# The last rows: each accumulator copied by two engines, and one transfer for each half over four batches

## Chip, cores and metric

The kernel runs on one core of a Trainium2 chip. Its time is the device time of one execution in microseconds (us). Times inside a profile count from the first instruction of the profiled execution.

## What is computed

There are 8 batches, each with 512 tokens and 32 state rows, in 8 heads of 64. The tokens read the state by attention and the state reads the tokens; the two results are put together as 544 rows of 512 for each batch. Every row then goes through the same two-layer network.

```python
scores = scale * np.matmul(x, state.transpose(0, 1, 3, 2))     # (8, 8, 512, 32)
xread = np.matmul(softmax(scores), state)                      # 512 rows of each batch
scores2 = scale * np.matmul(state, x.transpose(0, 1, 3, 2))    # (8, 8, 32, 512)
sread = np.matmul(softmax(scores2), x)                         # 32 rows of each batch
x = concatenate([xread, sread], axis=2) ...reshape(8 * 544, 512)
h = x @ w_in                                                   # (4352, 2048)
g = np.where(h <= -1, 0, np.where(h >= 1, h, (h + 1) ** 2 / 4))
out = g @ w_out                                                # (4352, 512), float32
```

Rows 544 b to 544 b + 511 of `out` are batch b's tokens, rows 544 b + 512 to 544 b + 543 its state rows.

## The kernel before

The kernel goes through nine steps: the tokens of batches 0 to 7, and then, as b = B = 8, the state rows of all eight batches together, 8 x 32 = 256 rows. In each step the hidden units are taken in groups. `g1` (line 504) makes a group's hidden values in PSUM and squares and bounds them on ScalarE and VectorE; `g2` (line 515) multiplies them with `w_out` and adds to accumulators of 128 rows x 512 columns (`acc[b][t]`), four for a batch's tokens and two (t = 0 and 1) for the state rows. Each product is done in three matmuls (lines 534 to 536) of values split in a high and a low part. The loop at line 807 does `g1` of a group, prepares the next one and then does `g2` of the group before; line 825 does the last `g2`.

In the last group of a step the matmuls are sorted by accumulator (line 525), so accumulator 0 is finished first, and `store` (line 542) is called as each is finished. In the last step that is 12 matmuls for accumulator 0, its `store`, 12 matmuls for accumulator 1, its `store`, and then the program ends. `store` copies the accumulator from PSUM into a tile `o` in SBUF and writes it to `out` by DMA. For tokens (b < 8) ScalarE copies, and one transfer of 128 rows goes out on ScalarE's own queue. For the state rows, accumulator t holds 32 rows of each of the batches 4 t to 4 t + 3, which lie 544 rows apart in `out`. Accumulator 0 is copied by ScalarE, accumulator 1 by VectorE (line 546), each as 512 columns, and then four transfers of 32 rows, 64 KB each, go out, two on ScalarE's queue (ACT) and two on SyncE's (SP).

The order of instructions on each engine is the order of the code in this part. A planner with costs (class `Plan`) orders only the first batch. Waits between engines are put in by the tile layer, which tracks the accesses of each tile. The end of the program (line 865) is SyncE waiting for the last transfers, and a drain of all engines.

Of the kernel before, what the change touches and what calls it, by code (L numbers as in the profile page):

```python
# [137 lines left out]
def state_exchange_moe(  # L138
# [17 lines left out]
    nc = tc.nc  # L156
    B, P, NT, H, D = x.shape
    S = NT * P
    NS = 32
    DM = H * D  # L160
# [6 lines left out]
    TOK = S + NS  # L167
# [283 lines left out]
    acc = {}  # L451
# [63 lines left out]
    def g2(b, j, half=None):  # L515
        n = n_of[b]
        per = S // n
        nt = n // P
        if b not in acc:
            acc[b] = [ps_acc(f"acc{b}_{t}") for t in range(nt)]  # L520
        gh, gl = gs[b, j]
        last = j == NJ // per - 1
        pairs = [(i, t) for i in range(2 * per) for t in range(nt)]
        if last:
            pairs.sort(key=lambda p: p[1])
        if half is not None:
            pairs = pairs[half * len(pairs) // 2:][:len(pairs) // 2]
        for i, t in pairs:
            f = 2 * per * j + i
            oh, ol = wo[f // 2][:, 0, f % 2], wo[f // 2][:, 1, f % 2]  # L530
            c0 = (i % per) * n + t * P
            lh, ll = (v[:, i // per, c0:c0 + P] for v in (gh, gl))
            a = acc[b][t]
            nc.tensor.matmul(a, lhsT=lh, rhs=oh, start=f == 0, stop=False)  # L534
            nc.tensor.matmul(a, lhsT=lh, rhs=ol, start=False, stop=False)  # L535
            nc.tensor.matmul(a, lhsT=ll, rhs=oh, start=False, stop=f == NF - 1)  # L536
            if last and i == 2 * per - 1:
                store(b, t)
# [3 lines left out]
    def store(b, t):  # L542
        if t == 0:
            outs[b] = rawp.tile([P, NT, DM], F32, tag="raw", name=f"o{b}")
        o = outs[b][:, t]
        if b == B and t % 2:
            nc.vector.tensor_copy(o, acc[b][t])
        else:
            nc.scalar.copy(out=o, in_=acc[b][t])  # L549
        if b < B:  # L550
            r0 = b * TOK + t * P
            nc.scalar.dma_start(out=out[r0:r0 + P, :], in_=o)
        else:
            for i in range(4):
                r0 = (4 * t + i) * TOK + S
                (nc.sync if i % 2 else nc.scalar).dma_start(
                    out=out[r0:r0 + NS, :], in_=o[i * NS:(i + 1) * NS]
                )

# [307 lines left out]
```

## Time and profile before

| | us |
|---|---|
| median of 3 runs | 663.96 (663.55 to 664.05) |
| the profiled execution | 664.0 |
| its span, first to last instruction | 662.2 |
| TensorE matmul busy | 653.9 |
| ScalarE / VectorE busy | 356.5 / 340.3 |
| HBM read / written | 34.08 MB / 8.91 MB |

The profile shows one execution. Engines are PE (TensorE matmul), PEld (its weight load), ACT (ScalarE), DVE (VectorE), POOL (GpSimd) and SP (SyncE); a q behind the name means the engine's sequencer, which issues DMAs and waits. A timeline row gives the start, the duration, the engine, the line of the kernel and the operation with its tiles; idle time before it and what ended it stand in brackets. A row of windows gives, for a stretch of time, each engine's busy time, the granted clock of TensorE, the mean busy share of the 16 DMA engines, and the GB/s that they moved. What ended an idle time is inferred by the profiler.

### The profile page before, as it was taken

How to read it: one execution, taken by the hardware profiler on the slowest of the kernel's cores; microseconds unless marked ns; L12 is line 12 of the kernel's file. 1: busy time of each engine (PE TensorE's matmuls, PEld its weight loads, DVE VectorE, ACT ScalarE, POOL GpSimd, SP SyncE). 2: the span in 40 equal slices, each digit the busy share in tenths (PEclk: the TensorE clock that was granted, in tenths of full speed). 3: DMA queues.
4: the chain of work that ended last, by engine and by line, in shares of the span. 5: the costliest groups of instructions: out<-in, count | busy, mean ns of one | idle time of the engine just before them, and what ended most of it. 6: DMA issues, size and time to landing. Idle time of an engine off the chain costs nothing.

```text
span 662.2 us, 10304 instructions
## 1 busy us (share of the span) xinstructions
PE 653.9 (99%) x4442; PEld 514.2 (78%) x4442; DVE 340.3 (51%) x490; ACT 356.5 (54%) x462; POOL 0.8 (0%) x7
## 2 busy tenths in 40 slices
PE   8999999999999999999999999999999999999997
PEld 6677777777787777777787777777778777778896
DVE  5999947623673239433563338433563343333431
ACT  4899847544554446544554447444653454454642
POOL 0000000000000000000000000000000000000000
PEclk9999999999999999999999999999999999999999
DMA  8986103010301003010301002010100000000101
GB/s 359 400 359 249 64 10 119 0 65 0 120 10 64 1 4 124 0 65 0 128 1 64 1 24 105 0 65 0 65 1 1 1 33 32 1 1 1 63 1 33
DMA packets 11085, 43.65 MB, mean 66 GB/s; under 512 B 1312, under 2 KB 1440, under 8 KB 7968
## 3 DMA queue, kind: packets, MB, share of 16 engines
q1 hardware_dynamic: 6096, 34.28, 13.6%
q10 hardware_dynamic: 4944, 8.72, 3.5%
q8 instruction: 35, 0.57, 0.3%
q14 instruction: 10, 0.08, 0.0%
HBM read 34.08 MB, written 8.91 MB: 65 GB/s over the span
## 4 chain that ended last, share of the span: by engine, by line
PE 91%; ACT 5%; DVE 3%; issue 0%; DMA 0%; POOL 0%; SPq 0%; ACTq 0%; POOLq 0%
PE acc L534 19%; PE acc L536 18%; PE acc L535 18%; PE h L477 9%; PE h L479 9%; PE h L478 9%; PE sw L417 5%; PE sc L253 1%; PE sr L350 1%; PE e2p L333 1%; PE warmed L198 1%; ACT u L482 1%; ACT u L485 1%; ACT raw_i L588 1%; DVE w L596 1%; ACT wo L603 0%
## 5 line engine op out<-in xcount | busy, mean ns | idle before, releaser
L534 PE MATMUL acc<-wo,gh 128*128 128x512 f32 x544 | 218.8, 402 | 0.0
L535 PE MATMUL acc<-wo,gh 128*128 128x512 f32 x544 | 212.3, 390 | 0.0
L536 PE MATMUL acc<-wo,gl 128*128 128x512 f32 x544 | 212.2, 390 | 0.0
L482 ACT ACTIVATE u<-h,half 128x512 f32<-128x512 f32 x136 | 93.7, 693 | 219.9 <-PE h L479 202.6
L488 DVE SCALAR_TENSOR_TENSOR u<-u,h 128x512 f32<-128x512 f32 x136 | 87.0, 680 | 206.7 <-ACT u L485 206.7
L534 PEld LDWEIGHTS acc<-wo,gh 128*128 128x128 f32 x544 | 102.1, 188 | 40.1 <-ACT u L482 12.8
L536 PEld LDWEIGHTS acc<-wo,gl 128*128 128x128 f32 x544 | 102.1, 188 | 22.5 <-issue 0.4
L535 PEld LDWEIGHTS acc<-wo,gh 128*128 128x128 f32 x544 | 102.2, 188 | 19.4 <-DVE wo L607 0.3
L502 DVE TENSOR_TENSOR gl<-u,gh 128x1024 fp32r<-128x1024 f32 x68 | 83.2, 1224 | 33.0 <-ACT gh L497 32.0
L497 ACT CAST gh<-u 128x1024 fp32r<-128x1024 f32 x68 | 71.8, 1056 | 50.3 <-DVE u L488 49.9
L485 ACT ACTIVATE u<-u 128x1024 f32<-128x1024 f32 x68 | 72.5, 1065 | 1.3
L417 PE MATMUL sw<-w,sb 64*32 64x256 f32 x1024 | 36.0, 383 | 1.8 <-DVE w L596 1.3
L417 PEld LDWEIGHTS sw<-w,sb 64*32 64x32 f32 x1024 | 15.1, 106 | 17.9 <-issue 8.8
L479 PE MATMUL h<-atl,sw_0h 128*128 128x512 f32 x60 | 23.6, 393 | 0.3 <-DVE atl L306 0.2
L477 PE MATMUL h<-ath,sw_0h 128*128 128x512 f32 x60 | 23.5, 394 | 0.0
L549 ACT COPY o<-acc 128x512 f32<-128x512 f32 x33 | 18.6, 586 | 9.1 <-PE acc L536 9.0
L478 PE MATMUL h<-ath,sw_0l 128*128 128x512 f32 x60 | 23.5, 391 | 0.0
L479 PE MATMUL h<-atl,sw_6h 128*128 128x512 f32 x60 | 23.4, 389 | 0.0
L479 PE MATMUL h<-atl,sw_2h 128*128 128x512 f32 x60 | 23.4, 389 | 0.0
L477 PE MATMUL h<-ath,sw_2h 128*128 128x512 f32 x60 | 23.3, 389 | 0.0
L478 PE MATMUL h<-ath,sw_2l 128*128 128x512 f32 x60 | 23.3, 389 | 0.0
L477 PE MATMUL h<-ath,sw_4h 128*128 128x512 f32 x60 | 23.3, 389 | 0.0
(174 smaller groups left out, 735.0 us busy)
## 6 DMA issues: line engine op xcount, KB each, us to landing
xt<-in_xt_dram SPq DMA_DIRECT2D x16, 512.0 KB, 4.5
raw_i<-in_moe_w_in_dram SPq DMA_DIRECT2D x8, 1024.0 KB, 6.9
raw_o<-in_moe_w_out_dram SPq DMA_DIRECT2D x8, 1024.0 KB, 9.4
xn<-in_x_dram SPq DMA_DIRECT2D x8, 1024.0 KB, 6.4
out_dram<-o ACTq DMA_DIRECT2D x32, 256.0 KB, 2.0
sb<-in_state_dram SPq DMA_DIRECT2D x1, 448.0 KB, 12.6
out_dram<-o SPq DMA_DIRECT2D x4, 64.0 KB, 1.7
out_dram<-o ACTq DMA_DIRECT2D x4, 64.0 KB, 2.0
```

The source lines that it names most:

```text
L417: nc.tensor.matmul(pt[pr * NS:(pr + 1) * NS, hh, i * CI:(i + 1) * CI], lhsT=sb[rows, b, pr], rhs=w32[c + i][rows, pr], start=True, stop=True,)
L477: nc.tensor.matmul(o, lhsT=wh[:, k, sl], rhs=ah[:, k], start=first, stop=False)
L478: nc.tensor.matmul(o, lhsT=wl[:, k, sl], rhs=ah[:, k], start=False, stop=False)
L479: nc.tensor.matmul(o, lhsT=wh[:, k, sl], rhs=al[:, k], start=False, stop=last)
L482: nc.scalar.activation(out=self.u[:, i], in_=self.hs[i], func=AF.Relu, scale=0.5, bias=half)
L485: nc.scalar.activation(out=self.u, in_=self.u, func=AF.Square)
L488: nc.vector.scalar_tensor_tensor(out=self.u[:, i], in0=self.u[:, i], scalar=1.0, in1=self.hs[i], op0=ALU.min, op1=ALU.max,)
L497: nc.scalar.copy(out=gh, in_=self.u)
L502: nc.vector.tensor_tensor(out=gl, in0=self.u, in1=gh.bitcast(F32), op=ALU.subtract)
L534: nc.tensor.matmul(a, lhsT=lh, rhs=oh, start=f == 0, stop=False)
L535: nc.tensor.matmul(a, lhsT=lh, rhs=ol, start=False, stop=False)
L536: nc.tensor.matmul(a, lhsT=ll, rhs=oh, start=False, stop=f == NF - 1)
```

## The change

Only `store` is changed, and in it only the last step. Both accumulators are treated alike: ScalarE copies columns 0 to 255 and VectorE columns 256 to 511. Each half is then written by one transfer of 128 KB, the left on ScalarE's queue and the right on SyncE's. `rows` is a view of `out` with the four batches outermost, then 32 rows, then the columns; the source side of a transfer is 128 partitions x 256 columns.

```diff
         o = outs[b][:, t]
-        if b == B and t % 2:
-            nc.vector.tensor_copy(o, acc[b][t])
-        else:
+        if b < B:
             nc.scalar.copy(out=o, in_=acc[b][t])
-        if b < B:
             r0 = b * TOK + t * P
             nc.scalar.dma_start(out=out[r0:r0 + P, :], in_=o)
         else:
-            for i in range(4):
-                r0 = (4 * t + i) * TOK + S
-                (nc.sync if i % 2 else nc.scalar).dma_start(
-                    out=out[r0:r0 + NS, :], in_=o[i * NS:(i + 1) * NS]
-                )
+            rows = out.rearrange("(b t) d -> b t d", b=B)[4 * t:4 * t + 4, S:S + NS]
+            lo, hi = slice(0, DM // 2), slice(DM // 2, DM)
+            nc.scalar.copy(out=o[:, lo], in_=acc[b][t][:, lo])
+            nc.vector.tensor_copy(o[:, hi], acc[b][t][:, hi])
+            nc.scalar.dma_start(out=rows[:, :, lo], in_=o[:, lo])
+            nc.sync.dma_start(out=rows[:, :, hi], in_=o[:, hi])
```

## Rows read from the trace of the kernel before

**Rows 1.** Page, busy time, share of the span and instructions of each engine.

```profile
PE 653.9 (99%) x4442; PEld 514.2 (78%) x4442; DVE 340.3 (51%) x490; ACT 356.5 (54%) x462; POOL 0.8 (0%) x7
```

**Rows 2.** Chain that ended last, the tail: start us, us, what.

```profile
656.37 1.70 DMA out_dram<-o
```

**Rows 3.** Timeline, end of each accumulator and its copy: start us, us, what.

```profile
654.92 0.39 PE L536 MATMUL acc<-wo,gl 128*128 128x512 f32 x1
...
655.35 0.59 ACT L549 COPY o<-acc 128x512 f32<-128x512 f32 x1 [3.96 <-PE acc L536]
...
657.64 0.39 PE L536 MATMUL acc<-wo,gl 128*128 128x512 f32 x1
658.07 0.69 DVE L547 COPY o<-acc 128x512 f32<-128x512 f32 x1 [5.42 <-DMA out_dram<-o]
```

**Rows 4.** Timeline, first and last DMA issue behind that copy.

```profile
658.78 0.32 SPq L556 DMA_DIRECT2D out_dram<-o  x1
...
659.20 0.44 ACTq L556 DMA_DIRECT2D out_dram<-o  x1
```

**Rows 5.** Windows: engines' busy us, then PEclk, DMA share and GB/s.

```profile
1.60:1.80 0.20, 0.20 (x1) 0.20 (x2) 0.00 (x0) 0.20 (x1) 0.00 (x0) 1.00 0.58 102
...
617.40:617.50 0.10, 0.10 (x2) 0.10 (x1) 0.10 (x1) 0.00 (x0) 0.00 (x0) 1.00 0.56 225
...
616.50:622.00 5.50, 5.50 (x39) 5.11 (x38) 2.29 (x3) 2.73 (x6) 0.00 (x0) 1.00 0.49 191
...
655.90:658.50 2.60, 2.13 (x10) 1.43 (x8) 0.43 (x1) 0.04 (x1) 0.00 (x0) 1.00 0.39 101
...
659.60:659.70 0.10, 0.00 (x0) 0.00 (x0) 0.00 (x0) 0.00 (x0) 0.00 (x0) 1.00 0.77 205
660.70:660.80 0.10, 0.00 (x0) 0.00 (x0) 0.00 (x0) 0.00 (x0) 0.00 (x0) 1.00 0.11 21
...
658.50:662.20 3.70, 0.00 (x0) 0.00 (x0) 0.26 (x1) 0.00 (x0) 0.00 (x0) 1.00 0.27 71
```

**Rows 6.** Line 865 from 659.75 us: durations in ns (min/median/max), first and last start.

```profile
L865 SPq EVENT_SEMAPHORE  x2: 207/730/1252, 659.7 to 661.0; - x2
```

**Rows 7.** Timeline of batch 7's stores: two copies in a row, the first issue.

```profile
615.97 1.07 ACT L549 COPY o<-acc 128x512 f32<-128x512 f32 x2
...
616.58 0.34 ACTq L552 DMA_DIRECT2D out_dram<-o  x1
```

**Rows 8.** Groups by line and shape: xcount | busy us, mean ns | idle before.

```profile
L549 ACT COPY o<-acc 128x512 f32<-128x512 f32 x33 | 18.6, 586 | 9.1 <-PE acc L536 9.0
L337 ACT COPY e<-e2p 128x1024 f32<-128x1024 f32 x8 | 8.1, 1015 | 0.0
...
L502 DVE TENSOR_TENSOR gl<-u,gh 128x1024 fp32r<-128x1024 f32 x68 | 83.2, 1224 | 33.0 <-ACT gh L497 32.0
L547 DVE COPY o<-acc 128x512 f32<-128x512 f32 x1 | 0.7, 692 | 5.4 <-DMA out_dram<-o 5.4
L260 DVE STREAM_TRANSPOSE z<-sc 128x256 f32<-128x256 f32 x4 | 1.6, 429 | 6.5 <-PE sc L253 6.5
```

**Rows 9.** Timeline at 48 us: two engines that read the scores of batch 1.

```profile
48.34 0.72 DVE L260 STREAM_TRANSPOSE z<-sc 128x512 f32<-128x512 f32 x1 [0.91 <-ACT e L322]
...
49.09 0.69 ACT L322 ACTIVATE e<-sc,nm 128x512 f32<-128x512 f32 x1 [0.78 <-DVE z L260]
```

**Rows 10.** DMA queues (SP is q1, ACT q10), and issues: xcount, KB, us to landing.

```profile
q1 hardware_dynamic: 6096, 34.28, 13.6%
q10 hardware_dynamic: 4944, 8.72, 3.5%
...
out_dram<-o ACTq DMA_DIRECT2D x32, 256.0 KB, 2.0
...
out_dram<-o ACTq DMA_DIRECT2D x4, 64.0 KB, 2.0
sb<-in_state_dram ACTq DMA_DIRECT2D x1, 64.0 KB, 4.3
```

## The prediction

> **What bounds the kernel now.** I read the page first: TensorE is busy for 653.9 us of a span of 662.2, so anything that leaves TensorE's work as it is can act only before its first or behind its last matmul [rows 1]. The change sits behind the last, so next come the chain of waits and the timeline of the last 8 us. The chain leaves TensorE early and goes through a copy, a DMA issue and a landing that ends at 658.07 into the last copy [rows 2], and the timeline names the same DMA as that copy's releaser. This has to be doubted. The last matmul of that accumulator runs 657.64 + 0.39 = 658.03, and the copy starts 0.04 us behind it, just as ScalarE's copy of the first accumulator starts 0.04 behind its own (654.92 + 0.39 = 655.31, copy at 655.35) [rows 3]. I take TensorE as the releaser.
>
> From there the tail is: VectorE's copy 658.07 to 658.76 [rows 3]; two transfers on each queue, the first issued at 658.78, the last at 659.20 [rows 4]; their data moves from about 659.61 to 660.8 [rows 5]; SyncE's two last waits for landings, 1.252 us from 659.7 and 0.207 from 661.0, end at 661.2 [rows 6]; the closing steps fill the rest to 662.2. So from the last data to the end of the span it is 1.4 us, 0.4 of them to the last landing. From an issue to its first data it is about 0.84: 658.78 to the slice at 659.60, and 616.58 to the slice at 617.40 for a store in mid-run [rows 5, 7]. The whole tail is 4.2 us.
>
> **The change, copies.** No copy of 256 columns is in the trace. ScalarE takes 586 ns for 512 columns and 1015 for 1024, 0.84 ns a column, so 0.37 us for 256. VectorE takes 692 for 512 and 1224 for 1024, 1.04 ns a column, so 0.43, and its 256-column transposes take 429 ns [rows 8]. Side by side both halves would be out by 658.50. But both read the same accumulator, and the trace has two such readers of one score tile: VectorE's transpose at 48.34 waits for ScalarE's exponential, and the next exponential at 49.09 for that transpose (48.34 + 0.72 = 49.06), though both only read the scores and write different tiles [rows 9]. So I put the halves one behind the other, ScalarE first as the code has it: ScalarE 658.07 to 658.44, VectorE 658.48 to 658.91. The left half is out 0.32 us earlier than now, the right 0.15 later. Bounds for the right half: 658.50 (together) and 658.91.
>
> **Issues.** Each accumulator has two transfers instead of four, so the second issue on each queue goes. An issue follows its copy by 0.02 us (658.76 to 658.78): ACT at 658.46, SP at 658.93, where the last is at 659.20 now. Their data can start at 659.30 and 659.77. First accumulator: ScalarE copies 655.35 to 655.72, issue at 655.74, data from 656.58; VectorE copies 655.76 to 656.19, issue at 656.21, data from 657.05. Behind these on ScalarE, VectorE and SP nothing is queued that TensorE needs: its remaining matmuls write the other accumulator, and both engines are idle until it ends.
>
> **Transfer.** This decides. Now a transfer moves 32 rows of 2 KB; then 128 half rows of 1 KB, and its write side counts four batches outermost and 32 rows within. First the price of a half row. Four stores of 128 full rows in mid-run take 0.49 of 5.5 us of 16 engines, 0.674 us each for eight rows per engine: 0.084 us a row. The last two accumulators, as many bytes in four transfers each, take 0.39 x 2.6 = 1.01 and 0.27 x 3.7 = 1.00 us [rows 5]: three more transfers cost 0.33, so closing one costs up to 0.11, and a row is 0.0705 to 0.084. A half row lies between half of the lower, 0.035, and the whole of the higher, 0.084. Long rows show little cost per row: SP's queue (34.28 MB in 6096 packets) and ACT's (8.72 MB in 4944) both come to some 42 ns of engine time per KB, 13.6% and 3.5% of 16 x 662.2 us [rows 10]. That would make a half row 0.042. The slice with the 512-byte rows of the state load has 0.58 x 0.2 x 16 = 1.86 engine-us for 20 KB, 91 ns per KB [rows 5], and a line through 512 bytes at that rate (0.046) and 2 KB at 0.082 gives 0.058. That slice holds the cold start of the loads too, so I take 0.048, nearer the lower.
>
> Second, over how many engines a transfer is dealt when four is outermost: no row shows it. Every transfer in the trace counts 128 or 32 outermost, which sixteen divides, and is closed on all sixteen: ACT's 32 + 4 + 1 = 37 transfers have 32 x 128 + 4 x 32 + 128 = 4352 rows, and its 4944 packets are 592 = 37 x 16 more [rows 10]. Four can't be dealt evenly over sixteen. The bounds are sixteen engines (the first rival) and, if each outermost step is one share, four; one engine, the far end, would give about 684 us by the sum below, and there is no reason for it. I take four. The Trainium skill, "DMA: Bandwidth & Descriptors", section "Why a DMA increments its semaphore by 16 and not by 1", has this as a rule: a transfer is split along the slowest dimension of each side, over the largest number up to 16 that divides both, and on these two queues over the lowest-numbered engines. By that rule the sum is the one that follows, without it the first rival's; this trace agrees as far as it goes (128 and 32 rows, sixteen engines) and has no case of four.
>
> On four engines a transfer gives each 32 half rows, and both queues' transfers share the same four: 64 x 0.048 + 2 x 0.11 = 3.29 us per accumulator, where now it is 1.0. First accumulator: 656.58 to 659.87. The second's data, ready at 659.30, queues behind it and ends at 659.87 + 3.29 = 663.16. The gains and losses in copies and issues drop out, as the four engines are never idle from 656.58 on. With 1.4 us behind it the span is 664.6, 2.4 more. The profiled execution took 664.0, 1.8 us around its span and 0.04 above the median of the runs shown: **666.4 us**. With half rows at 0.040 it is 665.3, at 0.058 667.6. The ends of the price give 665.0 (at 0.035 the first accumulator is out at 659.04, before the second arrives, and 659.30 + 2.46 = 661.76 ends the data) and 671.0.
>
> **Rivals.** (1) Sixteen engines, not slower: the second accumulator's left half moves 659.30 to 659.79 (8 x 0.048 + 0.11), the right 659.77 to 660.28, against 660.8 now: **663.5 us**, and 663.2 to 664.1 over the price of a half row and the two orders of the copies. For it: every transfer of the trace. Against: none has this shape. It decides from about eight engines upward. It can't gain 1.33 us: copy 0.37, issue 0.02, lag 0.84 and data of at least 0.3 end at 659.6 at best, 1.2 before now.
> (2) The transfer over four batches is issued as four after all, on both queues: from 658.93 on SP, 0.44 us apart as now [rows 4], the last at 660.25 instead of 659.20: **665.0 us**. Against: every store in the trace is one instruction.
> (3) The chain is right, and the second accumulator's copy waits for the landing of the first one's stores, as both lie in one tile. With four engines that is 659.87 + 0.4 = 660.27, copy 0.37, issue 0.02, data from 661.50 to 664.79: **668.0 us**. Against: in mid-run ScalarE copies two accumulators of one tile back to back, 615.97 to 617.04, and the first one's data moves only from 617.40 on [rows 5, 7].
>
> **Chances.** Four engines 0.71, sixteen 0.22, split again 0.03, the wait 0.04. A measurement of this kernel tells about 0.2%, 1.33 us, from no change, so 665.3 is the border. Of the four-engine case 0.82 lies above it (half rows dearer than 0.040); with the wait that makes slower 0.62. Same holds the rest of it (0.13), the split and nearly all of the sixteen engines: 0.36. Faster 0.02. The forecast's own range is 665.3 to 667.6. For 8 in 10 the range has to take in the sixteen engines, and reaches from 663.3 to 668.0; above lies only a half row nearly as dear as a whole one.
>
> **What would show it.** Four DMA issues of 128 KB in the tail. Packets: each queue loses 4 x (32 + 16) = 192 and gains 2 x 128 and the closing ones: 5016 for ACT and 6168 for SP if a transfer closes on four engines, 5040 and 6192 on sixteen. The DMA share of the tail stays near 0.25, without a gap, from 656.6 to 663; a share near 1.0 with a gap before 659.3 is rival 1 and makes the forecast wrong. VectorE's half copy starts 0.04 us behind the end of ScalarE's; if both start at 658.07, the turn-taking is wrong, at no price under four engines. TensorE's last matmul ends at 658.03 as now.

## The result: 1.94 us slower

The changed kernel takes 665.49 us (median of 7 runs, 664.98 to 666.12), the kernel before in the same series 663.55 (7 runs, 662.98 to 664.05). The ratio is 1.0031, 95% interval 1.002 to 1.0042: slower, by a little more than a measurement of this kernel can tell from no change. The profiled execution took 666.12 us, the slowest of the seven, with a span of 664.4, against 664.0 and 662.2.

The tail of the timeline answers [rows 3 and 4]: start, duration, engine, line, operation, and in brackets what ended the idle time before it.

```profile
655.58 1.15 ACTq L555 DMA_DIRECT2D out_dram<-o  x1
...
657.47 0.39 PE L536 MATMUL acc<-wo,gl 128*128 128x512 f32 x1
657.89 0.37 ACT L553 COPY o<-acc 128x256 f32<-128x256 f32 x1 [2.35 <-PE acc L536]
658.29 0.55 ACTq L555 DMA_DIRECT2D out_dram<-o  x1
658.30 0.42 DVE L554 COPY o<-acc 128x256 f32<-128x256 f32 x1 [2.29 <-ACT o L553]
658.75 0.54 SPq L556 DMA_DIRECT2D out_dram<-o  x1
```

TensorE ends at 657.47 + 0.39 = 657.86, 0.17 us earlier than before; so much the body of the program differs from one execution to the next. What the change does is best read from that point on. From the last matmul's end to the end of the span it was 4.17 us (658.03 to 662.2) and is 6.54 (657.86 to 664.4): 2.37 us more. I call this stretch the tail below.

The windows show where it goes, as in [rows 5]: stretch, engines' busy us, granted clock, share of the 16 DMA engines, GB/s.

```profile
656.80:657.50 0.70, 0.70 (x5) 0.55 (x3) 0.00 (x0) 0.00 (x0) 0.00 (x0) 1.00 0.19 29
657.50:662.70 5.20, 0.36 (x2) 0.00 (x0) 0.42 (x1) 0.37 (x1) 0.00 (x0) 0.93 0.27 95
...
662.90:663.10 0.20, 0.00 (x0) 0.00 (x0) 0.00 (x0) 0.00 (x0) 0.00 (x0) 0.50 0.05 15
663.10:663.30 0.20, 0.00 (x0) 0.00 (x0) 0.00 (x0) 0.00 (x0) 0.00 (x0) 0.50 0.00 0
```

For 5.2 us the DMA share stands at 0.27 and the rate at 95 GB/s, and there is no gap between the two accumulators. Before, the data of each took about 1.2 us, with an idle stretch between them. The data ends just before 663.1; the rest of the span behind it is 1.3 us.

The page's DMA queues say how many engines close a transfer; they answer [rows 10] (packets, MB, share).

```profile
q1 hardware_dynamic: 6168, 34.28, 13.5%
q10 hardware_dynamic: 5016, 8.72, 3.4%
```

These are 6096 - 192 + 264 and 4944 - 192 + 264: each of the four new transfers has 128 half rows and four closing packets, not sixteen. The share alone, 0.27 of sixteen, would be 4.3 engines; in the trace's DMA records a packet of 1 KB lasts 46 ns and the next one on the same engine begins 42 ns after it, so the records overlap a little.

The transfers of both queues run on the same four engines, one after the other: SyncE's first is issued at 656.03, but in the DMA records its data moves only from 658.63 on, as that of ScalarE's first ends.

### The profile page after: what moved, and what is told of

It is laid out like the page before. It is cut to its first block, busy times and chain, and to the rows that moved or that the text cites. A ratio compares the mean times of both kernels' runs of the same rounds, so it can differ in the third digit from the quotient of the medians.

```text
span 664.4 us, 10301 instructions
## 1 busy us (share of the span) xinstructions
PE 653.7 (98%) x4442; PEld 514.5 (77%) x4442; DVE 340.4 (51%) x491; ACT 356.5 (54%) x463; POOL 0.8 (0%) x7
## 3 DMA queue, kind: packets, MB, share of 16 engines
q1 hardware_dynamic: 6168, 34.28, 13.5%
q10 hardware_dynamic: 5016, 8.72, 3.4%
## 4 chain that ended last, share of the span: by engine, by line
PE 91%; ACT 5%; DVE 3%; issue 0%; POOL 0%; ACTq 0%; POOLq 0%
PE acc L534 19%; PE acc L536 18%; PE acc L535 18%; PE h L477 9%; PE h L478 9%; PE h L479 9%; PE sw L417 4%; PE sc L253 1%; PE sr L350 1%; PE e2p L333 1%; PE warmed L198 1%; ACT u L482 1%; ACT raw_i L586 1%; ACT u L485 1%; DVE w L594 1%; ACT gh L497 0%
## 5 line engine op out<-in xcount | busy, mean ns | idle before, releaser
L536 PE MATMUL acc<-wo,gl 128*128 128x512 f32 x544 | 212.3, 390 | 0.0
L536 PEld LDWEIGHTS acc<-wo,gl 128*128 128x128 f32 x544 | 102.2, 188 | 22.4 <-issue 0.4
L478 PE MATMUL h<-ath,sw_4l 128*128 128x512 f32 x60 | 23.4, 389 | 0.0
L477 PE MATMUL h<-ath,sw_6h 128*128 128x512 f32 x60 | 23.4, 389 | 0.0
```

The source lines that it names most:

```text
L477: nc.tensor.matmul(o, lhsT=wh[:, k, sl], rhs=ah[:, k], start=first, stop=False)
L478: nc.tensor.matmul(o, lhsT=wl[:, k, sl], rhs=ah[:, k], start=False, stop=False)
```

## Experiments

Each ratio is to the kernel before, timed in the same series on the same chip; e1 to e4, e5 to e9 and e10 to e13 were three series, on three chips. The tail is from one execution of each kernel, the profiled one. The packets are those of ScalarE's queue (ACT): 4944 before, less 192 for the old transfers, and for each new transfer on this queue its rows and one closing packet for each engine. For e4_eight that is 4944 - 192 + 2 x (128 + 8) = 5024.

| kernel | engines | ACT packets | tail, us | ratio to before (95%) |
|---|---|---|---|---|
| before | 16 | 4944 | 4.17 | 1 |
| the change | 4 | 5016 | 6.54 | 1.0031 (1.002 to 1.0042) |
| e2_two_batches | 2 | 5016 | 12.79 | 1.0125 (1.0112 to 1.0139) |
| e4_eight | 8 | 5024 | 4.76 | 1.0006 (0.9997 to 1.0015) |
| e3_sixteen | 16 | 5040 | 4.15 | 0.9998 (0.999 to 1.0007) |
| e5_copies | 16 | 4944 | 4.23 | 0.9999 (0.999 to 1.0007) |
| e6_one_store | 16 | 5040 | 4.81 | 1.0012 (1.0003 to 1.0021) |
| e1_full_rows | 4 | 4884 | 9.04 | 1.0068 (1.0056 to 1.0081) |
| e8_rows_two_queues | 4 | 4888 | 8.80 | 1.0069 (1.0057 to 1.0082) |
| e9_one_queue | 4 | 5280 | 6.61 | 1.0042 (1.0029 to 1.0056) |
| e10_rows_pitch48 | 4 | 4884 | 8.94 | 1.0068 (1.0051 to 1.0085) |
| e11_rows_pitch64 | 4 | 4884 | 9.03 | 1.0068 (1.0053 to 1.0083) |
| e12_change_pitch48 | 4 | 5016 | 6.47 | 1.003 (1.002 to 1.004) |
| e13_rows_of_tokens | 4 | 4884 | 8.88 | 1.0073 (1.0058 to 1.0088) |

### The outermost count: two, eight, sixteen

The theory is that the count of the outermost dimension on the write side sets how many DMA engines a transfer gets, and that four of them are the loss. The rival is that half rows of 1 KB, or scattered ones, cost so much. Three kernels keep the copies and the half rows and change only that count.

Two batches to a transfer:

```diff
-            nc.scalar.dma_start(out=rows[:, :, lo], in_=o[:, lo])
-            nc.sync.dma_start(out=rows[:, :, hi], in_=o[:, hi])
+            for i in range(2):
+                two, p = rows[2 * i:2 * i + 2], slice(i * 2 * NS, (i + 1) * 2 * NS)
+                nc.scalar.dma_start(out=two[:, :, lo], in_=o[p, lo])
+                nc.sync.dma_start(out=two[:, :, hi], in_=o[p, hi])
```

> As the change, but every half of an accumulator goes out in two transfers over two batches each. Engine count: two DMA engines, share about 0.125, 128 half rows per engine and accumulator, 128 x 0.045 + 4 x 0.1 = 6.2 us; the two accumulators from 656.7 to about 669, span about 670.4, 8 us slower than before, ratio 1.012. Rival (half rows cost, engine count plays no part): as the change or up to 0.5 us more for the second issue, ratio 1.003 to 1.004.

The ratio is 1.0125 and the tail 8.6 us longer than before; the packets are those of two closing ones for each of the eight transfers. The share is about an eighth, and so it stays:

```profile
660.00:668.40 8.40, 0.00 (x0) 0.00 (x0) 0.00 (x0) 0.00 (x0) 0.00 (x0) 0.50 0.14 48
```

For sixteen and eight the 256 state rows are kept in another order, so that the partitions of an accumulator run over rows and then batches, or batches and then 16 rows (the two places that fill and read `srT` follow suit and are not shown):

```diff
-    srT = const.tile([P, NPR, B, NS], F32, name="srT")
+    srT = const.tile([P, NPR, NS, B], F32, name="srT")     # e3; e4: [P, NPR, 2, B, NS // 2]
...
-            rows = out.rearrange("(b t) d -> b t d", b=B)[4 * t:4 * t + 4, S:S + NS]
+            rows = out.rearrange("(b t) d -> t b d", b=B)[S + 16 * t:S + 16 * t + 16]   # e3
+            rows = out.rearrange("(b t) d -> b t d", b=B)[:, S + 16 * t:S + 16 * t + 16]   # e4
```

> As the change, with the same copies and the same four transfers of 128 half rows, but the state rows are put in the order (row, batch) when they are kept, so that the write side counts 16 rows outermost and 8 batches within. Engine count: all 16 engines, share near 1.0 in two bursts, second accumulator's data from about 659.4 to 660.4, span about 661.8, 0.4 us faster than before, ratio 0.9994. Rival (half rows, or strided destinations, are what costs): as the change, ratio 1.003.

> As e3_sixteen, but the order is (half, batch, row), so that the write side counts 8 batches outermost and 16 rows within. Engine count: eight engines, share about 0.5, 32 half rows per engine and accumulator, 1.6 to 1.8 us; the first accumulator is out before the second comes at 659.4, whose data ends at about 661.2; span about 662.6, 0.4 us slower than before, ratio 1.0006. Rival (half rows cost, engine count plays no part): as the change, ratio 1.003.

Both follow the engine count. With sixteen the loss is gone, with the same bytes in the same half rows by the same four transfers; the 0.4 us of gain that I expected did not come (tail 4.15 against 4.17). The issue is at 657.99 and the first data at about 659.2, 1.2 us behind it instead of 0.84, and the data still takes nearly 1.2 us, not 1.0. With eight 0.59 us of the tail remain, which the ratio can't tell from none. The second accumulator's data, sixteen first, then eight with its slow beginning and its steady part:

```profile
658.00:659.20 1.20, 0.00 (x0) 0.00 (x0) 0.41 (x1) 0.00 (x0) 0.00 (x0) 1.00 0.00 0
659.20:660.40 1.20, 0.00 (x0) 0.00 (x0) 0.00 (x0) 0.00 (x0) 0.00 (x0) 1.00 0.76 219
```

```profile
659.50:660.00 0.50, 0.00 (x0) 0.00 (x0) 0.00 (x0) 0.00 (x0) 0.00 (x0) 1.00 0.40 70
...
660.20:661.20 1.00, 0.00 (x0) 0.00 (x0) 0.00 (x0) 0.00 (x0) 0.00 (x0) 1.00 0.55 193
```

The first row of e3 is the gap: its first accumulator is out long before the second is there, so nothing queues.

### The copies alone

```diff
-            nc.scalar.dma_start(out=rows[:, :, lo], in_=o[:, lo])
-            nc.sync.dma_start(out=rows[:, :, hi], in_=o[:, hi])
+            for i in range(4):      # four transfers of 32 whole rows, as before the change
```

> The copies of the change alone: both accumulators copied in two halves by ScalarE and VectorE, then four transfers of 32 whole rows each, as before the change. Turn-taking (my theory): VectorE's half starts 0.04 us behind the end of ScalarE's 0.37 us, all four transfers wait for it, 0.15 us slower than before, ratio 1.0002. Rival (the copies run together): both start 0.04 us behind the last matmul, 0.27 us faster, ratio 0.9996. The profile decides, the time can't. In both, 16 engines, share near 1.0, and nothing of the 2 us of the change.

The copies take turns, in this kernel as in the change:

```profile
657.30 0.37 ACT L552 COPY o<-acc 128x256 f32<-128x256 f32 x1 [2.35 <-PE acc L536]
657.71 0.42 DVE L553 COPY o<-acc 128x256 f32<-128x256 f32 x1 [2.29 <-ACT o L552]
```

The two halves read one accumulator and also write one tile; which of the two makes them take turns is not shown, though the readers in [rows 9] take turns and write different tiles. The tail is 0.06 us longer, the ratio 0.9999. So the copies neither gain nor lose anything that can be measured, and all of the loss belongs to the transfers.

### Whole rows on four engines: a miss

Copies as before, one transfer of whole rows over four batches for each accumulator:

```diff
-            for i in range(4):
-                ... four transfers of 32 rows
+            rows = out.rearrange("(b t) d -> b t d", b=B)[4 * t:4 * t + 4, S:S + NS]
+            (nc.sync if t % 2 else nc.scalar).dma_start(out=rows, in_=o)
```

> Copies as before the change (ScalarE all 512 columns of accumulator 0, VectorE of accumulator 1); each accumulator goes out in one transfer of 128 whole rows over four batches. Engine count (my theory: four batches outermost means four DMA engines): DMA share about 0.25 in the tail, first data about 656.9, 32 rows of 0.082 us per engine and a closing of 0.11 = 2.7 us per accumulator, the second from about 659.7 to 662.5, 1.4 us behind it: span 663.9, about 1.7 us slower than before, ratio 1.0025. Rival (the half rows of 1 KB are what costs, not the engine count): whole rows over 16 engines, share near 1.0, 0.3 us faster than before, ratio 0.9995.

The share and the closing packets, 4884 = 4944 - 192 + 128 + 4, say four engines, but the tail is 4.87 us longer than before, not 1.7. Windows of all its data, of its slow beginning, of the steady part, of the second accumulator's beginning and of the end:

```profile
657.10:665.80 8.70, 0.96 (x5) 0.46 (x3) 0.69 (x1) 0.00 (x0) 0.00 (x0) 0.84 0.21 60
657.30:658.90 1.60, 0.76 (x4) 0.30 (x2) 0.69 (x1) 0.00 (x0) 0.00 (x0) 1.00 0.24 22
659.50:661.50 2.00, 0.00 (x0) 0.00 (x0) 0.00 (x0) 0.00 (x0) 0.00 (x0) 1.00 0.26 101
661.60:662.60 1.00, 0.00 (x0) 0.00 (x0) 0.00 (x0) 0.00 (x0) 0.00 (x0) 1.00 0.26 63
664.50:665.70 1.20, 0.00 (x0) 0.00 (x0) 0.00 (x0) 0.00 (x0) 0.00 (x0) 0.50 0.06 24
```

The share is near a quarter from the start, but for 1.6 us the four engines move 22 GB/s, then 101. In the steady part that is 25 GB/s an engine, 2 KB in 0.081 us: the price that I had taken, and no more than on sixteen engines. At 101 GB/s all 524 KB would take 5.2 us; the data lasts from about 657.3 to 665.6. So what I missed is not the price of a row but 3 us in slow stretches: the two beginnings (in the first of them single rows last up to 0.86 us in the DMA records), and an end in which one engine, a sixteenth, works alone. Two kernels ask whether one queue at a time or whole rows are to blame. The first sends whole rows over both queues (64 partitions each, four batches outermost, with the rows kept in a fitting order), the second sends the change's half rows over one queue:

```diff
+            for h in range(2):                               # e8
+                rows = out.rearrange("(b t) d -> b t d", b=B)[4 * t:4 * t + 4, S + 16 * h:S + 16 * h + 16]
+                (nc.sync if h else nc.scalar).dma_start(out=rows, in_=o[64 * h:64 * h + 64])
...
-            nc.sync.dma_start(out=rows[:, :, hi], in_=o[:, hi])      # e9
+            nc.scalar.dma_start(out=rows[:, :, hi], in_=o[:, hi])
```

> Copies as before the change; state rows in an order (accumulator, half, batch, row) so that each accumulator goes out in two transfers of 64 whole rows, four batches outermost, one on each queue. Four engines in every theory. One queue is slow (a four-engine transfer starts slowly unless the other queue has data too): 32 rows x 0.082 + 0.2 = 2.85 us per accumulator, from 657.1 to 662.8, span 664.2, 2.0 us slower than before, ratio 1.003. Whole rows are slow on four engines: as e1_full_rows, 4.4 us slower, ratio 1.0067.

> As the change, with both halves of each accumulator issued on ScalarE's queue. Four engines in every theory. One queue is slow: 1.5 to 2 us more than the change, ratio about 1.006. Whole rows are slow: as the change, ratio 1.003.

Whole rows stay slow over two queues (tail 8.80), and half rows stay as fast as in the change over one (6.61 against 6.54; the ratios, from two series, have intervals that overlap). So it is not the queues: it goes with the whole rows, or with the whole-width copies that both slow kernels also have. Half rows are not free of such stretches either: on two engines, in e2_two_batches, the rate falls from 44 GB/s in 657.0 to 658.2 to 26 in 658.2 to 660.0. Four more kernels move the place that is written, and leave the state rows' own places unwritten, to see whether the distance between the four groups is behind it:

```diff
-            rows = out.rearrange("(b t) d -> b t d", b=B)[4 * t:4 * t + 4, S:S + NS]
+            rows = out[:B * 48].rearrange("(b t) d -> b t d", b=B)[4 * t:4 * t + 4, :NS]   # e10, e12; e11: 64
+            rows = out.rearrange("(b t) d -> b t d", b=B)[4 * t:4 * t + 4, 0:NS]           # e13
```

> As e1_full_rows (whole rows, one transfer over four batches for each accumulator), but the state rows are written over rows of batch 0, with 48 rows from one group of 32 to the next instead of 544; their own places in the output are left unwritten. Four engines in every theory. From the last matmul's end to the end of the span it is 4.17 us before the change and 9.03 in e1_full_rows. Place (whole rows were slow because of where the four engines write, 544 rows apart): 32 x 0.0825 + 0.1 = 2.75 us per accumulator, the tail 6.0 us, ratio 1.0028. Size (whole rows are slow on four engines wherever they go): tail 9.0, ratio 1.0067.

> As e10_rows_pitch48 with 64 rows, 128 KB, from group to group. Place, and a power of two is worse: slower than e10_rows_pitch48, tail 9 us or more. Place, and only the 544 rows matter, or rows that were written before are fast: tail 6.0. Size: tail 9.0.

> As the change, but the state rows are written over rows of batch 0 with 48 rows from group to group, as in e10_rows_pitch48. Place: the slow first 0.6 us of the change (36 GB/s instead of 97) goes, tail 6.0 to 6.2 us instead of 6.54, ratio 1.0027. Size: as the change, tail 6.5, ratio 1.0031.

> As e1_full_rows, but the state rows are written over the first 32 token rows of each batch, which were written long before: the same 544 rows from group to group. Their own places are left unwritten. Place by distance: as e1_full_rows, tail 9.0, ratio 1.0067. Rows that were written before are fast: tail 6.0, ratio 1.0028. Size: tail 9.0.

None of it matters: 8.94, 9.03 and 8.88 us with whole rows, 6.47 with half rows. Of the places tried none made whole rows fast, and none removed a loss in the half rows. Why transfers of whole rows on four engines begin so slowly and end so unevenly stays open.

### One store for each accumulator

The shortest tail seemed to be one copy and one transfer of whole rows on sixteen engines, with the row order of e3_sixteen:

```diff
+        nc.scalar.copy(out=o, in_=acc[b][t])                  # both accumulators
...
+            rows = out.rearrange("(b t) d -> t b d", b=B)[S + 16 * t:S + 16 * t + 16]
+            nc.scalar.dma_start(out=rows, in_=o)
```

> State rows in the order (row, batch) as in e3_sixteen, ScalarE copies all 512 columns of both accumulators, and each goes out in one transfer of 128 whole rows, 16 rows outermost and 8 batches within, on ScalarE's queue. Engine count: 16 engines; last copy 658.07 to 658.66, issue 658.68, data from about 659.6 to 660.4, span 661.8, 0.4 us faster than before, ratio 0.9994, as e3_sixteen. Rival (one transfer on one queue starts slowly, which is what made e1_full_rows 4.4 us slower instead of 1.7): 1.5 us more, ratio 1.0017.

Neither: the tail is 0.64 us longer than before, the ratio 1.0012. Its data takes 1.2 us (0.78 of 16 engines in 659.40 to 660.60, below), as before, but the first comes 1.2 us behind the issue at 658.24 instead of 0.84, as in e3_sixteen, and from the last data to the end it is 1.7 us instead of 1.4. No kernel of this study beats the one before.

```profile
658.24 0.56 ACTq L552 DMA_DIRECT2D out_dram<-o  x1
```

```profile
659.40:660.60 1.20, 0.00 (x0) 0.00 (x0) 0.00 (x0) 0.00 (x0) 0.00 (x0) 1.00 0.78 218
```

## Why the prediction was right

The forecast was 2.4 us more, 666.4; the tail grew by 2.37, the profiled execution took 666.12, and the medians differ by 1.94. The changed kernel's median, 665.49, lies 0.9 us under the forecast; half of that is the base, the 664.0 of one execution, where the median of seven is 663.55. Point by point:

- **Releaser.** The chain of before named a DMA as releaser of the last copy [rows 2, 3]; I took TensorE. In the changed kernel the copy of the second accumulator starts 0.03 us behind TensorE while the first one's data is on its way until about 660: it waits for no landing. e1_full_rows, with the old copies, has the same row with TensorE in the bracket (5.44 <-PE acc L536). The third rival is out.
- **Copies.** 0.37 and 0.42 us against 0.37 and 0.43, one behind the other with 0.04 between them. Their price is nothing, as said, but the reason I gave (a backlog) is only half of it: on sixteen engines, in e5_copies, it is 0.06 us.
- **Engines.** Four: the packets, 5016 and 6168, are the numbers written down for four, and the share is 0.27 without a gap. With two, eight and sixteen outermost the closing packets, the share and the tail follow. The rule of the Trainium skill, "DMA: Bandwidth & Descriptors", section "Why a DMA increments its semaphore by 16 and not by 1", held at all four counts; which of the sixteen engines they were, no run here shows. The first rival is out, and so is the second: there are four issues.
- **The price of a half row and of a closing.** 0.048 us was taken for the one and 0.11 for the other, 128 x 0.048 + 4 x 0.11 = 6.58 us in all. At 95 GB/s four engines move 23.8 GB/s each, 1 KB in 0.043, and that rate holds the closings already: 524 KB take 5.5 us. So the sum had about 1.06 us too much, 0.6 in the half rows and nearly all of the 0.44 in the closings. In the DMA records a closing packet is 4 bytes and lasts 9 ns. The 0.11 came from the 0.33 us of engine time that four small transfers took more than one large one; by these records it was not the closings; what it was stays open.
- **The start.** I let the first data follow its issue by 0.84 us, at 656.58. It comes at about 656.9, 1.3 behind the issue at 655.58, and until 657.5 it moves 29 GB/s instead of 95. From 656.58 to 657.5 that is 0.92 us for 20 KB, which take 0.21 at 95 GB/s: 0.71 us were missing.
- **The end.** The four engines don't finish together: behind 662.7 the rate is down, and in 662.9 to 663.1 it is 15 GB/s. At 95 GB/s to the end the data would have been out at about 662.8; it is out at about 663.05, and this 0.2 us was missing too.

So 0.9 us too little and 1.06 too much nearly cancel: the data ends at 663.05 instead of 663.16. The mechanism was right, four engines on which the second accumulator's data queues behind the first's. That the sum came so near was luck: its errors each way were over a third of the 2.4 us that it forecast.

## What to carry to other kernels

Joining small transfers saves issues, but look at what the join puts outermost: here it took four of sixteen DMA engines and cost more than it saved, and putting a dimension that sixteen divides outermost gave the loss back. The number of closing packets in a queue tells how many engines a transfer ran on. A sum of bytes at the steady rate is a lower bound: e1_full_rows has the steady rate that I had reckoned with and still takes 3 us more, in slow beginnings and in an end with one engine at work.

## What the runs showed of the hardware that I had not expected

- In the steady part the price of a row hardly depends on how many engines carry it: whole rows cost 0.0705 to 0.084 us each on sixteen by the working of the prediction and 0.081 on four in e1_full_rows, half rows 0.043 on four. What differs is the beginnings: 29 GB/s for 0.6 us in the change, 70 instead of 193 for 0.5 us in e4_eight, 22 instead of 101 for 1.6 us in e1_full_rows.
- An issue of these transfers takes 0.54 to 0.55 us, and the first on each queue more (1.15 and 0.70), where the stores of 128 rows in mid-run take 0.34 [rows 7]. The minimum, median and maximum in ns:

```profile
L555 ACTq DMA_DIRECT2D out_dram<-o x2: 552/850/1148, 655.6 to 658.3; - x2
L556 SPq DMA_DIRECT2D out_dram<-o x2: 542/620/698, 656.0 to 658.7; - x2
```

The data comes later too: 1.2 to 1.3 us behind the start of the issue in the change, e3_sixteen and e6_one_store, where it was 0.84 before. In the change that counts once, in the start above, as the second issue lies beside the first accumulator's data. Whether the longer issue is what makes the data late is not shown.
